# Weights of a two-layer linear-attention kernel asked for behind a copy on POOL, the last key sums one chunk later, and a layer norm's transposes all on DVE

## The chip, the cores and the metric

The kernel runs on one core of a Trainium2 chip. The time is the device time of one execution in microseconds (us), the median of several. Before the change three runs gave 2497.05 us as the median, 2494.74 to 2499.38.

## The reference

A row matrix x of 2048 x 576 goes through two layers, each an attention block and a dense block, with the same weights in both layers:

```
x = x + A(layernorm(x))      # 32 heads of 18: q, k, v = x @ wqkv
                             # phi(p) = [softmax(p), softmax(-p)], p = q @ w_phi or k @ w_phi, per head
                             # o = phi_q (phi_k^T v) / (phi_q . sum(phi_k) + 1e-6);  A = o @ wo
x = x + B(layernorm(x))      # h = relu(x @ w1 + b1)^2 (4608 wide);  B = h @ w2 + b2
```

All of it is float32. phi_k^T v and the sum of phi_k run over all 2048 rows, so a layer's attention outputs cannot begin before all of its keys are done.

## The kernel before, in words

**Numbers.** Each operand of a matrix product is split into a high part (rounded to fp32r) and a low part (the rest), and three products (high x high, high x low, low x high) stand for one. So each weight is held as two pieces, and PE (TensorE, the matmul engine) does nearly all of the work.

**Tiles and stages.** The rows come in four blocks of 512, each of four row tiles of 128. The kernel folds w_phi into the query and key weights, makes the keys of all blocks (`opening`), and then runs the dense blocks of the row blocks one after the other, in layer 0 in the order 3, 2, 0, 1 (tiles m_3, m_2, m_0, m_1), then `between` and layer 1. A dense block (`g_mlp`) loops over 36 chunks of 128 hidden features. A chunk f has 14 matmuls into ph (L975, the hidden layer), ReLU and square on ACT (ScalarE) into a tile hr (L980, L981; tag "hr", two buffers), a split of hr on DVE (VectorE) into hb (L984, L985), and, one chunk later, 12 matmuls by rows (L1000) and 3 for the last 128 columns (L992) into the accumulators. The chunk's weights come from DRAM through SP's DMA queue: m_h (640 KB, L938) into two buffers, asked for when the chunk two before has used its buffer, and m_s (576 KB, L950) likewise.

**What is woven in.** Between the steps of a dense block other work is put: a `Plan` holds calls with a turn and a depth, and `weave` runs one slot of it after each of the block's 72 yields. Turn n is slot 2n + 1, so about one turn passes for each chunk. In layer 0's dense block i the plan holds (a) for i < 3 the attention of the next row block (`plan_attend`): attention weights, their way through DRAM and back ("trips": stored by ACT's DMA queue as small pieces, fetched again in another order, and turned in 32 x 32 blocks by DVE, tiles z, phs and e), the output projection `out.project` (L816) with the output weights "o", and the layer norm of its result; and (b) for i > 0 the keys and values of layer 1 for the row block just finished (`plan_keys`): a layer norm, key products with weights "k" from turn 4 on, value products with weights "v" from turn 4.5 on, and the sums phi_k^T v (`kv_tile`, L593, 64 short matmuls a row tile) at turns 8.5 (row tiles 0 and 1) and 10.5 (2 and 3).

**How weights are asked for.** `asked` (L302) makes the calls that load a weight: four pieces, two halves times high and low, each one DMA on SP's queue (two for "o": the first four head groups, and a small one for the last), into tiles of two buffers for each of two tags. Key and output weights share the tags "wraw" and "rr" (TAGS_C); value weights share "whi" and "wlo" (TAGS_A) with the trips of blocks i > 0. The programs of PE, ACT, DVE and POOL (GpSimd) stand in the order in which they are written. SP's does not: its order is settled when the program is built, by when each DMA's buffer and data are reckoned to be ready, and on the chip it is kept. So a load whose buffer has long been free is issued early, and an issue that has to wait holds all behind it.

**The layer norm's transposes.** In the attention of blocks i > 0 and of layer 1 the normalised rows go through DRAM as well (`TripNorm`: DRAM tiles xrm, and xrt for the last 64 columns): `store` (L419, L422) and `fetch` (L430, L432) on ACT's queue, `flip` (L437) on DVE. In layer 0's first dense block only three of the four row tiles do, without their last 64 columns; the fourth tile and all four tails are transposed by PE (`Norm.turn` L384, `Norm.rest` L393, tiles a_2np).

## Time and profile before

| | |
|---|---|
| median of three runs | 2497.05 us (2494.74 to 2499.38) |
| the profiled execution, time | 2497.19 us |
| its span, first to last instruction | 2495.5 us |
| PE busy | 2478.5 us, 99% |
| DVE, ACT, POOL busy | 1260.1, 788.1, 189.4 us |
| moved by DMA | 545.07 MB, 218 GB/s on the mean |
| granted PE clock | 1.00 |

How to read the rows that follow in the prediction. A list of waits gives: engine, tile and line, "<-" who ended the wait, us in total, how many times, the longest. A timeline row gives the start, how long it took, engine, line, operation, out<-in tiles, and, in brackets, the engine's idle time before it and who ended it. A chain row gives a start and a length. A row of windows gives the stretch, its length, the busy time of PE, PEld (PE's weight loads), DVE, ACT and POOL (each with its count), the granted clock, the DMA engines' busy share and GB/s. SPq and ACTq are the DMA issues of those engines' queues; "issue" means that the engine waited for nothing that the profile shows. PE's ends are modelled, and a matmul starts before the modelled end of the one ahead of it.

### The profile page before, as it was taken

Reading aid. Unit: us, or ns where it says so; the run is one execution under the profiler, and the core shown is the slowest. Engines: PE = TensorE matmul, PEld = TensorE weight load, DVE = VectorE, ACT = ScalarE, POOL = GpSimd, SP = SyncE. Lnnn points to the kernel's source line nnn. Section 1 sums busy time; section 2 is a strip of 40 time slices with the busy share of each in tenths; the row PEclk is TensorE's granted clock in tenths of the full one; section 3 lists DMA queues with packets and bytes.
Section 4 is the critical chain, followed back from the end, with each engine's and each line's share of the span. In section 5 each row is a group of like instructions: output and inputs, shape, how many; then the busy total and the mean of one; then the engine's idle time right before and its main releaser. Section 6 shows DMA issues by size and latency. Waiting matters only on the chain.

```text
span 2495.5 us, 37635 instructions
## 1 busy us (share of the span) xinstructions
PE 2478.5 (99%) x14968; PEld 2182.9 (87%) x14968; DVE 1260.1 (50%) x2214; ACT 788.1 (32%) x1439; POOL 189.4 (8%) x539
## 2 busy tenths in 40 slices
PE   9999999999999999999999999999999999999999
PEld 8999888888888888888888988888888888888887
DVE  6679885545744476455113776433453436442112
ACT  5444453422232223223213332413233222312212
POOL 4211100000200001000000011000110002000000
PEclk9999999999999999999999999999999999999999
DMA  9313698986767677684565248678576867676565
GB/s 321 98 54 92 243 315 266 310 315 205 259 229 271 217 206 273 216 298 146 195 199 182 92 141 263 209 217 291 186 257 204 261 219 246 217 230 230 194 199 171
DMA packets 214374, 545.07 MB, mean 218 GB/s; under 512 B 29006, under 2 KB 96814, under 8 KB 214198
## 3 DMA queue, kind: packets, MB, share of 16 engines
q1 hardware_dynamic: 163638, 500.44, 60.8%
q10 hardware_dynamic: 50560, 42.21, 5.3%
q8 instruction: 119, 1.95, 0.3%
q14 instruction: 57, 0.47, 0.1%
HBM read 439.20 MB, written 103.38 MB: 217 GB/s over the span
## 4 chain that ended last, share of the span: by engine, by line
PE 95%; DMA 2%; DVE 1%; ACT 1%; issue 1%; SPq 0%; ACTq 0%; DVEq 0%
PE m_1ph L975 9%; PE m_3ph L975 9%; PE m_0ph L975 9%; PE m_2ph L975 9%; PE m_1acc L1000 7%; PE m_3acc L1000 7%; PE m_2acc L1000 7%; PE m_0acc L1000 7%; PE m_1acc L992 2%; PE m_3acc L992 2%; PE m_2acc L992 2%; PE m_0acc L992 2%; PE a_0po L816 1%; PE a_2po L816 1%; PE kvp L593 1%; PE a_3po L816 1%
## 5 line engine op out<-in xcount | busy, mean ns | idle before, releaser
L975 PE MATMUL m_2ph<-a_2nh,m_2h 128*128 128x512 f32 x720 | 225.2, 394 | 1.2 <-ACT m_2hr L980 0.7
L975 PE MATMUL m_0ph<-a_0nh,m_0h 128*128 128x512 f32 x720 | 225.0, 394 | 1.3 <-ACT m_0hr L980 1.1
L1000 PE MATMUL m_3acc<-m_3s,m_3hb 128*128 128x448 f32 x864 | 189.3, 367 | 0.4 <-DVE m_3hb L984 0.4
L1000 PE MATMUL m_1acc<-m_1s,m_1hb 128*128 128x448 f32 x864 | 189.0, 367 | 0.3 <-PE m_1ph L975 0.3
L1000 PE MATMUL m_2acc<-m_2s,m_2hb 128*128 128x448 f32 x864 | 188.9, 367 | 0.0
L1000 PE MATMUL m_0acc<-m_0s,m_0hb 128*128 128x448 f32 x864 | 188.8, 367 | 0.0
L984 DVE CAST m_2hb<-m_2hr 128x512 fp32r<-128x512 f32 x72 | 31.2, 433 | 292.4 <-ACT m_2hr L981 292.3
L1000 PEld LDWEIGHTS m_1acc<-m_1s,m_1hb 128*128 128x128 f32 x864 | 161.9, 188 | 18.8 <-PE m_1ph L975 0.5
L1000 PEld LDWEIGHTS m_3acc<-m_3s,m_3hb 128*128 128x128 f32 x864 | 161.2, 188 | 17.8 <-PE m_3ph L975 0.6
L1000 PEld LDWEIGHTS m_2acc<-m_2s,m_2hb 128*128 128x128 f32 x864 | 161.6, 188 | 17.2
L1000 PEld LDWEIGHTS m_0acc<-m_0s,m_0hb 128*128 128x128 f32 x864 | 161.6, 188 | 17.2
L975 PEld LDWEIGHTS m_2ph<-a_2nh,m_2h 128*128 128x128 f32 x720 | 135.3, 188 | 32.7 <-ACT m_2hr L980 1.2
L975 PEld LDWEIGHTS m_0ph<-a_0nh,m_0h 128*128 128x128 f32 x720 | 135.2, 188 | 32.8 <-ACT m_0hr L980 1.5
L984 DVE CAST m_1hb<-m_1hr 128x512 fp32r<-128x512 f32 x72 | 30.7, 427 | 258.8 <-ACT m_1hr L981 258.8
L980 ACT ACTIVATE m_2hr<-m_2ph,b1t 128x512 f32<-128x512 f32 x72 | 49.6, 689 | 339.1 <-PE m_2ph L975 327.4
L980 ACT ACTIVATE m_1hr<-m_1ph,b1t 128x512 f32<-128x512 f32 x72 | 49.6, 689 | 319.1 <-PE m_1ph L975 309.1
L980 ACT ACTIVATE m_0hr<-m_0ph,b1t 128x512 f32<-128x512 f32 x72 | 49.6, 689 | 317.2 <-PE m_0ph L975 288.6
L984 DVE CAST m_0hb<-m_0hr 128x512 fp32r<-128x512 f32 x72 | 31.5, 438 | 229.0 <-ACT m_0hr L981 229.0
L984 DVE CAST m_3hb<-m_3hr 128x512 fp32r<-128x512 f32 x72 | 31.7, 440 | 173.6 <-ACT m_3hr L981 173.6
L980 ACT ACTIVATE m_3hr<-m_3ph,b1t 128x512 f32<-128x512 f32 x72 | 49.6, 689 | 219.3 <-PE m_3ph L975 209.2
L975 PE MATMUL m_3ph<-t0onh,m_3h 128*128 128x512 f32 (+1 forms) x380 | 112.9, 384 | 0.6 <-ACT t0onh L385 0.5
L975 PE MATMUL m_1ph<-t1onh,m_1h 128*128 128x512 f32 (+1 forms) x380 | 112.4, 382 | 0.8 <-ACT t1onh L385 0.5
(2050 smaller groups left out, 5734.9 us busy)
## 6 DMA issues: line engine op xcount, KB each, us to landing
m_2h<-dw SPq DMA_DIRECT2D x72, 640.0 KB
m_0h<-dw SPq DMA_DIRECT2D x72, 640.0 KB
m_1h<-dw SPq DMA_DIRECT2D x72, 640.0 KB
m_2s<-dw SPq DMA_DIRECT2D x72, 576.0 KB
m_0s<-dw SPq DMA_DIRECT2D x72, 576.0 KB
m_1s<-dw SPq DMA_DIRECT2D x72, 576.0 KB
dw<-m_3h SPq DMA_DIRECT2D x36, 640.0 KB
m_3h<-dw SPq DMA_DIRECT2D x36, 640.0 KB
```

The source lines that it names most:

```text
L593: nc.tensor.matmul(po[32 * q : 32 * q + 32, :, j], vt[:, h * VW : h * VW + 32], e[:, :, h * DH : (h + 1) * DH], start=not stay, stop=True, ...
L816: nc.tensor.matmul(pt[:, :HP], a, m[:w, g], start=(g == 0 and k == 0), stop=(g == NG - 1 and k == 2))
L975: nc.tensor.matmul(ph[:, cols], a, m, start=(k == 0), stop=(k == 3 * KC + 1))
L980: nc.scalar.activation(hr, ph, AF.Relu, bias=b1t[:, f : f + 1])
L984: nc.vector.tensor_copy(hh, hr)
L992: nc.tensor.matmul(acc[KC], a, m, start=(f == 0 and k == 0), stop=(f == NF - 1 and k == 2))
L1000: nc.tensor.matmul(acc[t][:, :R], a[:, rows], m, start=(f == 0 and k == 0), stop=(f == NF - 1 and k == 2))
```

## The change

Four edits.

1. `asked` gets a flag `paced`. With it, ahead of each piece's DMA POOL copies one number into the piece's tile, from `beat["now"]`, the hr tile that was squared last. The DMA writes over that number, so it may not start before the copy, and the copy not before the square. It is on for "o" in layer 0's blocks i > 0 and for all key and value weights of `plan_keys`. The copy touches the first column of the first head group only, so the small DMA of each "o" piece has nothing to wait for.
2. The key weights of `plan_keys` for the third and fourth block are asked for at turns 32 to 35 of the block before (`keyw`), and then the value weights at turns 0 to 3 (8 to 11 in the last block, as before). In the second block both are asked for in its own first turns, as before.
3. The second sum of keys moves from turn 10.5 to 11.5.
4. In layer 0's first dense block all four row tiles and their tails now go through DRAM and DVE. Their fetches stand two turns later than before; the fourth tile is scaled sooner.

```diff
+    beat = {}
+
-    def asked(which, name, tags=TAGS_A):
+    def asked(which, name, tags=TAGS_A, paced=False):
...
+            if paced:
+                nc.gpsimd.tensor_copy(pair[half][k][0:1, 0, 0:1], beat["now"][0:1, 0:1])
             for d, piece in moved(which, half, k, pair[half][k]):
                 nc.sync.dma_start(piece, d)
...
-        trips = range(NT if whole else NT - 1)
-        norm = TripNorm(dst, f"{name}n", b, out.keep, trips, whole)
-        more = 0 if queries else 2
-        scales = [at + 1, at + 2, at + 3, at + 4 if whole else at + 5.5 + more]
+        norm = TripNorm(dst, f"{name}n", b, out.keep, range(NT), True)
+        more = 0 if queries else 2 if whole else 4
+        scales = [at + 1, at + 2, at + 3, at + 4]
...
             nc.vector.tensor_sub(hl, hr, hh.bitcast(F32))
+            beat["now"] = hr
...
-                        o = asked("o", n2, TAGS_C)
+                        o = asked("o", n2, TAGS_C, not layer)
...
+                        keyw = asked("k", f"w1_{b}", TAGS_C, True)
+                        for n, call in enumerate(keyw[1]):
+                            plan.put(at + 20.5 + n, 9, call)
...
-        (vw, vcalls), (kw, kcalls) = asked("v", f"w{m}"), asked("k", f"w{m}", TAGS_C)
+        vw, vcalls = asked("v", f"w{m}", TAGS_A, True)
+        kw, kcalls = keyw or asked("k", f"w{m}", TAGS_C, True)
         for n in range(4):
-            plan.put(8 + n if last else 2 + n / 2, 9, vcalls[n])
-            plan.put(n / 2, 9, kcalls[n])
+            plan.put(8 + n if last else n if keyw else 2 + n / 2, 9, vcalls[n])
+            if not keyw:
+                plan.put(n / 2, 9, kcalls[n])
...
-                plan.put(8.5 + t // 2 * 2, 3, add, t)
+                plan.put(8.5 + t // 2 * 3, 3, add, t)
```

What this moves, at three places of the programs. First SP's queue at the head of layer 0's second dense block. m_2h_4 is chunk 4's w1 weight, m_2s_3 chunk 3's w2 weight; w_3k0l is the low piece of the first half of the key weights, w_3v1h the high piece of the second half of the value weights. Before:

```order
L938 DMA m_2h_2_6316<-dw_2_143 128x1280
L938 DMA m_2h_3_6339<-dw_3_144 128x1280
L950 DMA m_2s_2_6318<-dw_2_179 128x1152
L310 DMA w_3k1l<-kept_kl 128x1440
L938 DMA m_2h_4_6403<-dw_4_145 128x1280
L310 DMA w_3v0l<-kept_vl 128x1440
L950 DMA m_2s_3_6378<-dw_3_180 128x1152
L310 DMA w_3v1h<-kept_vh 128x1440
L938 DMA m_2h_5_6462<-dw_5_146 128x1280
```

After the change:

```order
L941 DMA m_2h_2_6318<-dw_2_143 128x1280
L941 DMA m_2h_3_6343<-dw_3_144 128x1280
L314 DMA w_3k0h<-kept_kh 128x1440
L953 DMA m_2s_2_6320<-dw_2_179 128x1152
L314 DMA w_3k0l<-kept_kl 128x1440
L314 DMA w_3k1h<-kept_kh 128x1440
L314 DMA w_3k1l<-kept_kl 128x1440
L953 DMA m_2s_3_6383<-dw_3_180 128x1152
L314 DMA w_3v0h<-kept_vh 128x1440
L941 DMA m_2h_4_6409<-dw_4_145 128x1280
```

Before, m_2h_4 has one key piece ahead of it behind m_2s_2 (three key pieces and a value piece stood in the block before); now it has three key pieces, m_2s_3 and a value piece there, and the first key piece stands ahead of m_2s_2.

The same place in POOL's program (n_3d is the layer norm's reciprocal deviation of one row tile, two operations each). Before:

```order
L359 TENSOR_SCALAR n_3d_6284<-n_3m_6283 128x1
L360 TENSOR_TENSOR n_3d_6284<-n_3d_6284,mhalf 128x1
L359 TENSOR_SCALAR n_3d_6292<-n_3m_6291 128x1
L360 TENSOR_TENSOR n_3d_6292<-n_3d_6292,mhalf 128x1
L359 TENSOR_SCALAR n_3d_6335<-n_3m_6334 128x1
L360 TENSOR_TENSOR n_3d_6335<-n_3d_6335,mhalf 128x1
L359 TENSOR_SCALAR n_3d_6399<-n_3m_6398 128x1
L360 TENSOR_TENSOR n_3d_6399<-n_3d_6399,mhalf 128x1
```

After the change:

```order
L312 CAST w_3k0h<-m_2hr_6272 1x1
L363 TENSOR_SCALAR n_3d_6286<-n_3m_6285 128x1
L364 TENSOR_TENSOR n_3d_6286<-n_3d_6286,mhalf 128x1
L363 TENSOR_SCALAR n_3d_6294<-n_3m_6293 128x1
L364 TENSOR_TENSOR n_3d_6294<-n_3d_6294,mhalf 128x1
L312 CAST w_3k0l<-m_2hr_6272 1x1
L312 CAST w_3k1h<-m_2hr_6272 1x1
L363 TENSOR_SCALAR n_3d_6339<-n_3m_6338 128x1
L364 TENSOR_TENSOR n_3d_6339<-n_3d_6339,mhalf 128x1
L312 CAST w_3k1l<-m_2hr_6360 1x1
L312 CAST w_3v0h<-m_2hr_6360 1x1
```

The copies stand between the norms of the row tiles: the second and third piece behind the norms of two tiles, the fourth behind that of the third. The first three read the square of chunk 1 (m_2hr_6272), the next two that of chunk 2.

Last SP's queue where the output weights come in the second block (a_0o0h is the high piece of the first half; 126x1152 is the DMA of the first four head groups, 72x288 the small one). Before:

```order
L310 DMA a_0o0h<-kept_oh 72x288
L310 DMA a_0o0l<-kept_ol 126x1152
L938 DMA m_2h_10_6999<-dw_10_151 128x1280
L310 DMA a_0o0l<-kept_ol 72x288
L1491 DMA a_0qs_7404<-qs_3_128 128x576
L310 DMA a_0o1h<-kept_oh 126x1152
L950 DMA m_2s_9_6986<-dw_9_186 128x1152
L310 DMA a_0o1h<-kept_oh 72x288
L310 DMA a_0o1l<-kept_ol 126x1152
L938 DMA m_2h_11_7122<-dw_11_152 128x1280
L310 DMA a_0o1l<-kept_ol 72x288
```

After the change:

```order
L314 DMA a_0o0h<-kept_oh 126x1152
L314 DMA a_0o1h<-kept_oh 72x288
L953 DMA m_2s_13_7356<-dw_13_190 128x1152
L941 DMA m_2h_15_7423<-dw_15_156 128x1280
L314 DMA a_0o0l<-kept_ol 126x1152
L953 DMA m_2s_14_7408<-dw_14_191 128x1152
L314 DMA a_0o1l<-kept_ol 72x288
L941 DMA m_2h_16_7491<-dw_16_157 128x1280
L314 DMA a_0o1h<-kept_oh 126x1152
L953 DMA m_2s_15_7482<-dw_15_192 128x1152
L941 DMA m_2h_17_7548<-dw_17_158 128x1280
L314 DMA a_0o1l<-kept_ol 126x1152
```

Before, the pieces stood around m_2h_10 and m_2h_11, as soon as the key weights' buffers were free; now each large one stands behind another chunk's m_2h, from chunk 14's on. The small pieces of the high and low first half stay where they were.

8 lines of the change are left out of this document (4 added, 4 removed).

## Prediction

> **What bounds the kernel now.** I read the page first, then the list of waits of the matmul engine PE, then the places in the timeline that the list points to, and last the DMA windows.
>
> ```profile
> span 2495.5 us, 37635 instructions
> ## 1 busy us (share of the span) xinstructions
> PE 2478.5 (99%) x14968; PEld 2182.9 (87%) x14968; DVE 1260.1 (50%) x2214; ACT 788.1 (32%) x1439; POOL 189.4 (8%) x539
> ```
>
> PE is the bound: 2495.5 - 2478.5 = 17.0 us of the span are not matmuls. So a change that leaves the matmuls alone can win at most what PE waits. The change touches layer 0's dense blocks, and its weight loads lie between 520 and 1110 us (second and third dense block). The waits of PE in that window, all of them:
>
> ```profile
> PE kv_3k L593 <- issue: 1.2, 1, 1.2
> PE m_0ph L975 <- ACT m_0hr L980: 1.1, 1, 1.1
> PE m_2ph L975 <- ACT m_2hr L980: 0.7, 1, 0.7
> PE m_2ph L975 <- DMA m_2h<-dw: 0.5, 1, 0.5
> PE m_0ph L975 <- DMA m_0h<-dw: 0.2, 1, 0.2
> ```
>
> Five waits, 3.7 us in all. A listed wait is shorter than what it costs, since a matmul normally starts before the modelled end of the one ahead of it. In PE's timeline, the step from the last matmul group of one feature chunk to the next chunk, once without and once with a wait:
>
> ```profile
> 613.90 0.86 PE L992 MATMUL m_2acc<-m_2hb,m_2s 128*128 128x512 f32 x3
> 614.61 0.39 PE L975 MATMUL m_2ph<-a_2nh,m_2h 128*128 128x512 f32 x1
> ...
> 620.25 0.85 PE L992 MATMUL m_2acc<-m_2hb,m_2s 128*128 128x512 f32 x3
> 621.62 0.47 PE L975 MATMUL m_2ph<-a_2nh,m_2h 128*128 128x512 f32 x1 [0.51 <-DMA m_2h<-dw]
> ```
>
> The step takes 0.71 us without and 1.37 us with: 0.66 us lost for 0.51 listed, so 0.15 more for each wait. Five waits cost 3.7 + 5 x 0.15 = 4.5 us. That is what the paced loads can win.
>
> **Where those waits come from.** Mean DMA share and GB/s (last two columns) of five stretches:
>
> ```profile
> 533.00:541.50 8.50, 8.50 (x42) 7.31 (x41) 4.88 (x13) 2.86 (x5) 1.97 (x11) 1.00 1.02 403
> 594.00:622.00 28.00, 27.49 (x266) 24.01 (x266) 20.33 (x28) 9.07 (x14) 0.00 (x0) 1.00 0.97 261
> 610.00:615.00 5.00, 5.00 (x146) 4.53 (x146) 4.60 (x8) 2.67 (x4) 0.00 (x0) 1.00 1.00 239
> 636.00:662.00 26.00, 26.00 (x120) 22.20 (x120) 23.77 (x35) 7.16 (x10) 5.89 (x19) 1.00 0.82 271
> 776.00:789.00 13.00, 13.00 (x69) 11.62 (x69) 7.37 (x16) 2.40 (x4) 0.79 (x2) 1.00 1.01 357
> ```
>
> From 594 to 622 the four output-weight pieces arrive in one go on full DMA engines (0.97): the hidden weights m_2h come late at 621.62, and the 1.2 us named "issue" (PE waits for no semaphore) falls at 627, just behind the same jam. The third block's 0.2 us is the same place. From 776 to 789 three key pieces arrive on full engines (1.01), and ACT is held there (first the chain of waits, then ACT's timeline):
>
> ```profile
> 789.04 10.64 DMA xrm<-a_0nr
> ```
> ```profile
> 800.86 0.69 ACT L980 ACTIVATE m_2hr<-m_2ph,b1t 128x512 f32<-128x512 f32 x1 [6.62 <-issue]
> ```
>
> ACT may fetch the rows only when their store has landed, 10.64 us after its issue, at 799.7; the ReLU queued behind the fetch (L980) starts late, at 800.86, and PE waits 0.7 us for it (1.1 us in the third block).
>
> **The change part by part.** *All rows by DVE* (first dense block only). PE loses its transposes of the fourth row tile and of the tails. Their places in PE's timeline:
>
> ```profile
> 474.86 0.60 PE L384 MATMUL a_2np<-ident,a_2nn 128*128 128x128 f32 x4
> 475.29 0.38 PE L393 MATMUL a_2np<-ident,a_2ne 128*64 128x128 f32 x2
> 475.43 2.72 PE L1000 MATMUL m_3acc<-m_3s,m_3hb 128*128 128x448 f32 x12
> ```
>
> From start to start that is 0.57 us, and the other tail pair (0.14, as here from 475.29 to 475.43) makes 0.7 us. What comes instead, four small stores, two fetches and the 32x32 transposes, is on ACT's queue and DVE, which the page shows at 32% and 50%; the fetch now stands five turns behind its store, so ACT should not be held by it. If that cover failed, one ACT wait like the one above would come back, 0.9 us. *Key sums later* moves 64 short matmuls behind the next hidden chunk: same matmuls, no saving, no cost.
>
> *Output and key weights in pieces.* The output pieces move from the jam at 594 to four chunks from about 636 on, one per chunk; the key pieces of the third and fourth block come one per chunk behind the ReLUs of chunks 32 to 35, so that from 776 to 789 two 720 KB pieces fewer arrive. With both jams gone all five waits should go: -4.5 us. Bounds: -1.0 (only the two DMA waits, 0.7 + 2 x 0.15) to -4.5.
>
> *The head of the second block* pays. There all eight key and value pieces now come in the first chunks, where four came ahead of the block before. Each piece waits for POOL, POOL for the layer norm's sums, and SP's queue stands still meanwhile. What POOL does there (the norms of row tiles 1 and 2), ACT's square of chunk 2, which the fourth piece's copy reads, and two issues on SP's queue, chunk 4's m_2h and chunk 3's m_2s:
>
> ```profile
> 532.06 0.65 POOL L360 TENSOR_TENSOR n_3d<-n_3d,mhalf 128x1 f32<-128x1 f32 x1
> ...
> 534.89 0.64 POOL L360 TENSOR_TENSOR n_3d<-n_3d,mhalf 128x1 f32<-128x1 f32 x1
> ```
> ```profile
> 534.39 0.63 ACT L981 ACTIVATE m_2hr<-m_2hr 128x512 f32<-128x512 f32 x1
> ```
> ```profile
> 533.67 0.32 SPq L938 DMA_DIRECT2D m_2h<-dw  x1
> ...
> 536.80 0.32 SPq L950 DMA_DIRECT2D m_2s<-dw  x1
> ```
>
> The first key piece goes after chunk 1's square. The second and third stand behind the norm of two row tiles: 532.06 + 0.65 = 532.7, with a copy and the issue about 533.0. The fourth stands behind the next tile's norm and chunk 2's square (535.5), then m_2s_3, which is not free before 536.8, the first value piece, and only then m_2h_4: about 537.6 instead of 533.67. Sizes, in KB of 1024 bytes:
>
> ```profile
> m_2h<-dw SPq DMA_DIRECT2D x3, 640.0 KB
> m_2s<-dw SPq DMA_DIRECT2D x3, 576.0 KB
> w_3k1l<-kept_kl SPq DMA_DIRECT2D x1, 720.0 KB
> ```
>
> From 533.0 the queue has four pieces, m_2s_3 and m_2h_4 to move: 4 x 720 + 576 + 640 = 4096 KB = 4.19 MB. At the 403 GB/s of 533 to 541.5 that takes 10.4 us, up to 543.4. To this comes the time that a lone DMA needs beyond its bytes: SP's wait for the landing of a 288 KB store,
>
> ```profile
> SPq L1062 <- DMA xm<-a_0x: 7.2, 3, 3.0
> ```
>
> is 2.4 us on the mean, its bytes 0.7 us, and the issue is a little ahead, so about 2 us (an estimate). m_2h_4 lands near 545.4. PE wants it where it starts chunk 4, and the same chunk in the third block:
>
> ```profile
> 544.01 0.47 PE L975 MATMUL m_2ph<-a_2nh,m_2h 128*128 128x512 f32 x1
> ```
> ```profile
> 835.27 0.47 PE L975 MATMUL m_0ph<-a_0nh,m_0h 128*128 128x512 f32 x1
> ```
>
> That is a new wait of 1.4 us at 403 GB/s, and of 2.7 us at the 357 of the other full stretch (4.19 MB in 11.7 us). The 1.3 MB of the first piece and m_2s_2, issued from about 529 on, may not quite be through by 533.0, up to 0.7 us more. Between 1.4 and 3.4 I take 2.3 us: the 403 row is these very loads, with some of the rest. Behind chunk 4 come key products, which need no m_2h, so the delay is paid once. In the third block only value pieces come at the head: two of them, m_0s_3 and m_0h_4 are 2656 KB = 2.72 MB from about 824.3 on (291.3 us later than 533.0), 6.7 us and 2 us, landing at 833 to 834: no wait, 0 to 1.
>
> *The copies themselves.* 32 copies of one element; POOL's nearest rows are copies of 64 and of 8 columns:
>
> ```profile
> 634.51 0.24 POOL L727 COPY a_0z<-a_0Q0e 128x64 f32<-128x64 f32 x1
> 634.68 0.19 POOL L728 COPY a_0z<-a_0Q0e 128x8 f32<-128x8 f32 x1
> ```
>
> POOL is 8% busy. The number read (hr) has two buffers, so ACT's ReLU two chunks later waits for the copy; the longest queue ahead of a copy is the rearranging of one tile's weights (12 operations, at the 636 to 662 row's 5.89 / 19 = 0.31 us each 3.7 us) against two chunks, 12.7 us (614.61 to 621.62, less the 0.66 lost, twice). I cost this at nothing; if a copy came late by more than that cover, PE would wait for the ReLU.
>
> **The sum.** -4.5 - 0.7 + 2.3 = -2.9 us. The profiled execution took 2497.19 us, 0.14 above the median of 2497.05, so the forecast is 2497.05 - 2.9 = 2494.2 us. Two timings of this kernel can be told apart from about 0.2% (5 us) on; the runs shown spread over 4.6 us.
>
> **The rivals.** *The head drains in time.* If PE is not kept waiting at chunk 4, only the gains stay: -5.2, 2491.9 us, just past 0.2%. For it: single stretches at 533 to 541.5 ran above 403; against it: m_2h_4 is issued four us later with four pieces ahead. [...]
>
> *The output weights meet the attention trips.* From 636 to 662 the engines already carry 271 GB/s at share 0.82, mostly stores and fetches of attention weights. Four pieces of 648 KB add 2.65 MB in 26 us, 102 GB/s: 373 in all, share 1.1 at that stretch's own efficiency. A queue of up to 0.13 x 26 = 3.4 us would build, against a slack that the list of waits does not show. If it cost 1.5 us in each block: -2.9 + 3.0, 2497.2 us.
>
> *The jam only moves, and is dearer (slower).* If the eight pieces at the head drain like the output pieces did, at the 239 GB/s of 610 to 615, m_2h_4 needs 17.5 us and lands at 552.5: a wait of 8.5 us, and in the third block 11.4 us, 837.7, 2.4 us. Then 10.9 - 5.2 = +5.7, 2502.8 us. It decides from 10.2 us of new waits on, a drain below 245 GB/s. Against it: key and value pieces did move at 403 before; it is the output pieces that are slow.
>
> *It does not do what it says.* The "issue" wait and the two ReLU waits stay where they are: 3.0 + 3 x 0.15 = 3.5 us less gain, +0.6, 2497.6 us. For it: none of the three names a weight load. [...]
>
> **How the numbers follow.** Forecast 0.36, head drains in time 0.24, output weights collide 0.15, jam dearer 0.12, no effect on the three waits 0.13. Faster by over 0.2% is the first rival, 0.24; slower by over 0.2% the third, 0.12; the other cases lie within, 0.64. The range leaves out the jam: its low end is 2491.9 less the 1.4 us by which a gain could be sized too small, 2490.5; its high end is the collision or the no-effect case with the new wait at 3.4 instead of 2.3 us and 1 us in the third block, 2500.0.
>
> **What would show it.** Right: the five waits missing from PE's list, none at 594 to 630, and one new wait of 1 to 4 us for m_2h at chunk 4 of the second block; no a_2np matmuls. Wrong: PE waiting for ReLUs behind POOL's copies, a wait for m_2h or m_2s at chunks 14 to 18, or ACT still held ten us by the last row fetch.

## The result and the profile after

The change is slower. Four runs of the kernel after have a median of 2513.03 us (2511.48 to 2515.34), four of the kernel before 2496.68 us (2494.74 to 2499.38): a ratio of 1.0065, with a 95% interval from 1.0048 to 1.0083. The forecast was 2494.2, its range ended at 2500.0. The profiled execution took 2514.03 us, and its page begins:

```profile
span 2512.3 us, 37716 instructions
...
PE 2483.8 (99%) x14960; PEld 2184.4 (87%) x14960; DVE 1265.8 (50%) x2217; ACT 789.6 (31%) x1439; POOL 198.0 (8%) x571
```

PE has eight instructions fewer than before and yet is busy 5.3 us longer (2483.8 against 2478.5), and outside its matmuls the span is 28.5 us instead of 17.0. So there are two losses, waits and slower matmuls. PE's waits in the kernel after (lines have moved by 3 or 4: L978 is the hidden matmuls, L983 the ReLU, L1004 the second matmuls by rows, L996 those for the last 128 columns):

```profile
PE m_2ph L978 <- DMA m_2h<-dw: 3.2, 1, 3.2
PE m_2ph L978 <- ACT m_2hr L983: 3.2, 2, 2.5
PE m_0ph L978 <- ACT m_0hr L983: 2.6, 2, 1.4
PE m_2acc L996 <- DMA m_2s<-dw: 1.6, 1, 1.6
PE m_0acc L1004 <- DVE m_0hb L987: 1.6, 2, 0.8
...
PE m_2acc L1004 <- DMA m_2s<-dw: 1.0, 1, 1.0
```

The first is the wait that the prediction expected at the head. The "issue" wait at 627 us is gone; the waits for ReLUs are longer than before, and waits for feature pieces and for DVE have joined them. Three transfers now stand in the chain of waits of the second block, with their start and length:

```profile
537.69 9.45 DMA m_2h<-dw
...
657.54 16.58 DMA phs<-a_0z
...
812.00 6.62 DMA m_2s<-dw
```

The stretches that the prediction showed, in the kernel after (the last three columns are granted clock, DMA share, GB/s):

```profile
533.00:541.50 8.50, 8.50 (x43) 7.35 (x42) 4.73 (x13) 3.10 (x5) 2.39 (x6) 1.00 0.97 350
594.00:622.00 28.00, 28.00 (x275) 25.00 (x275) 18.49 (x24) 8.16 (x13) 0.00 (x0) 1.00 0.48 154
636.00:662.00 26.00, 26.00 (x211) 22.32 (x201) 20.92 (x29) 7.18 (x10) 7.40 (x28) 1.00 0.92 287
776.00:789.00 13.00, 13.00 (x76) 11.91 (x76) 6.79 (x17) 1.32 (x2) 0.79 (x2) 1.00 0.77 253
```

The bytes moved as planned: the jam of 594 to 622 went from share 0.97 to 0.48, that of 776 to 789 from 1.01 to 0.77, and 636 to 662 filled from 0.82 to 0.92 on the mean.

**Where the time went, by place.** I cut the second and the third dense block at the start of PE's hidden matmuls of chunks 9, 13 and 21 and took the lengths from PE's timeline of one profiled execution of each kernel. The pieces are the head (chunks 0 to 8), the stretch of the old jam (9 to 12), the attention trips (13 to 20) and the rest, with the block's end (21 to 35). First the lengths before, then the differences to before, in us; the last column is the measured ratio less one, times 2497 us.

```
                second block                third block               whole
                head  jam trips  end        head  jam trips  end      run
before          86.1 30.7  51.1 123.5       86.1 28.9  51.1 124.1
after           +5.0 -2.1  +6.1  +1.7       +1.4 -0.3  +4.4  +0.7    +16.2
all_free        +1.5 -1.8   0.0  -1.2        0.0 +1.0   0.0  -1.8     -0.7
pace_only       +6.2 -2.1  +7.5  -1.2       +5.0 -0.3  +6.8  -1.8    +18.5
o_free          +5.9 -2.1   0.0  +1.8       +0.4 -0.4   0.0  +0.8     +6.7
kv_free         +1.8 -2.0  +8.2  +0.2        0.0 -0.3  +3.4   0.0     +4.7
keyw_free       +3.2 -2.1  +4.2  -1.2       +1.2 -0.3  +3.5  -1.8    +10.0
copy_const      +5.8 -2.1  +0.3  -1.2       +0.7 -0.4  +1.3  -1.4     +4.2
pool_issue      +0.5 -2.0  +7.6  +0.7       +0.1 -0.3  +6.5  -0.6    +13.7
head_act        +3.3 -2.1  +6.8  +1.1       +1.2 -0.4  +4.5  +0.5    +14.7
warm16          +3.4 -2.1  +7.9  +4.8       +0.8 -0.3  +4.0  +0.7    +14.2
o_late          +6.7 -2.0   0.0  +5.2       +0.5 -0.3   0.0  +1.4     +7.0
late_free       +1.9 -2.1   0.0  +0.1        0.0 -0.3   0.0  -1.2     -2.5
before_late     -0.1 -2.1   0.0  +0.5        0.0 -0.3   0.0  -0.6     -0.7
sums_only       -0.1 -1.6   0.0  +0.5        0.0 +0.9   0.0  +0.2     +0.5
rows_only       +2.1 -2.1   0.0  +0.5        0.0 +0.2   0.0  -0.9     +0.2
late_best       -0.1 -2.2   0.0  -1.2        0.0 -0.3   0.0  -0.6     -2.2
```

In the kernel after, the eight pieces sum to 16.9 us. The first dense block is 0.7 us shorter (259.3 to 258.6), and the layers behind are as they were (1393.6 and 1393.7 us from the fourth block on). Three places lose: head, trips, end. One profile of a kernel is one execution: *o_free*, *keyw_free* and *o_late* below have the same program in the second block's head as the kernel after, and that head runs from +3.2 to +6.7 in the four profiles; the second block's trips, with the same program in *after*, *kv_free*, *keyw_free*, *head_act* and *warm16*, run from +4.2 to +8.2. So only differences beyond such a spread are read from the table.

**The slower matmuls.** At two places the granted clock is halved. Ahead of and behind the wait at the head, and ahead of and behind the wait of 2.5 us at 676:

```profile
544.70:548.00 3.30, 0.72 (x3) 0.66 (x4) 1.66 (x4) 0.01 (x1) 0.00 (x0) 1.00 1.01 421
548.10:551.40 3.30, 3.30 (x9) 2.63 (x8) 0.00 (x0) 0.00 (x0) 0.00 (x0) 0.50 1.02 420
674.40:677.70 3.30, 1.30 (x6) 1.07 (x7) 1.86 (x3) 2.37 (x3) 0.00 (x0) 1.00 0.77 216
677.80:681.10 3.30, 3.30 (x10) 2.53 (x9) 3.23 (x4) 0.00 (x0) 0.00 (x0) 0.50 0.99 340
```

Each costs about 1.6 us more: eight matmuls at 0.20 us over their usual step (0.43 instead of 0.23 us from one start to the next). Nothing of this kind was in the kernel before, or in the prediction.

### The profile page after: what moved, and what is told of

It is laid out like the page before. It is cut to its first block, busy times and chain, and to the rows that moved or that the text cites. A ratio compares the mean times of both kernels' runs of the same rounds, so it can differ in the third digit from the quotient of the medians.

```text
span 2512.3 us, 37716 instructions
## 1 busy us (share of the span) xinstructions
PE 2483.8 (99%) x14960; PEld 2184.4 (87%) x14960; DVE 1265.8 (50%) x2217; ACT 789.6 (31%) x1439; POOL 198.0 (8%) x571
## 4 chain that ended last, share of the span: by engine, by line
PE 92%; DMA 4%; issue 2%; DVE 1%; ACT 1%; POOL 0%; SPq 0%; ACTq 0%; DVEq 0%; POOLq 0%
PE m_1ph L978 9%; PE m_3ph L978 9%; PE m_2ph L978 9%; PE m_0ph L978 8%; PE m_1acc L1004 7%; PE m_3acc L1004 7%; PE m_2acc L1004 6%; PE m_0acc L1004 6%; PE m_1acc L996 2%; PE m_3acc L996 2%; PE m_2acc L996 2%; PE m_0acc L996 2%; PE a_2po L820 1%; PE a_0po L820 1%; DMA phs<-a_0z 1%
## 5 line engine op out<-in xcount | busy, mean ns | idle before, releaser
L978 PE MATMUL m_2ph<-a_2nh,m_2h 128*128 128x512 f32 x720 | 227.6, 398 | 6.5 <-DMA m_2h<-dw 3.2
L978 PE MATMUL m_0ph<-a_0nh,m_0h 128*128 128x512 f32 x720 | 225.1, 394 | 3.7 <-ACT m_0hr L983 2.6
L1004 PE MATMUL m_0acc<-m_0s,m_0hb 128*128 128x448 f32 x864 | 189.5, 367 | 1.7 <-DVE m_0hb L987 1.6
L1004 PE MATMUL m_2acc<-m_2s,m_2hb 128*128 128x448 f32 x864 | 189.3, 367 | 1.1 <-DMA m_2s<-dw 1.0
L1004 PE MATMUL m_3acc<-m_3s,m_3hb 128*128 128x448 f32 x864 | 189.3, 367 | 0.4 <-DVE m_3hb L987 0.4
L1004 PE MATMUL m_1acc<-m_1s,m_1hb 128*128 128x448 f32 x864 | 189.0, 367 | 0.4 <-PE m_1ph L978 0.4
L1004 PEld LDWEIGHTS m_0acc<-m_0s,m_0hb 128*128 128x128 f32 x864 | 161.3, 188 | 20.3 <-DVE m_0hb L987 2.5
L1004 PEld LDWEIGHTS m_1acc<-m_1s,m_1hb 128*128 128x128 f32 x864 | 161.9, 188 | 18.8 <-PE m_1ph L978 0.5
L1004 PEld LDWEIGHTS m_2acc<-m_2s,m_2hb 128*128 128x128 f32 x864 | 161.4, 188 | 19.2 <-issue 1.4
L1004 PEld LDWEIGHTS m_3acc<-m_3s,m_3hb 128*128 128x128 f32 x864 | 161.4, 188 | 18.0 <-PE m_3ph L978 0.6
L978 PEld LDWEIGHTS m_2ph<-a_2nh,m_2h 128*128 128x128 f32 x720 | 136.8, 190 | 38.7 <-ACT m_2hr L983 4.1
L978 PEld LDWEIGHTS m_0ph<-a_0nh,m_0h 128*128 128x128 f32 x720 | 135.2, 188 | 35.4 <-ACT m_0hr L983 3.4
L983 ACT ACTIVATE m_2hr<-m_2ph,b1t 128x512 f32<-128x512 f32 x72 | 49.6, 689 | 335.9 <-PE m_2ph L978 309.4
L983 ACT ACTIVATE m_1hr<-m_1ph,b1t 128x512 f32<-128x512 f32 x72 | 49.6, 689 | 321.2 <-PE m_1ph L978 316.2
L983 ACT ACTIVATE m_0hr<-m_0ph,b1t 128x512 f32<-128x512 f32 x72 | 49.6, 689 | 309.6 <-PE m_0ph L978 295.8
L983 ACT ACTIVATE m_3hr<-m_3ph,b1t 128x512 f32<-128x512 f32 x72 | 49.6, 689 | 216.8 <-PE m_3ph L978 206.7
L978 PE MATMUL m_2ph<-a_2nl,m_2h 128*128 128x512 f32 x288 | 114.0, 396 | 0.0
L978 PE MATMUL m_3ph<-t0onh,m_3h 128*128 128x512 f32 (+1 forms) x380 | 112.9, 384 | 0.6 <-ACT t0onh L389 0.5
```

Source lines behind the costliest of these rows:

```text
L978: nc.tensor.matmul(ph[:, cols], a, m, start=(k == 0), stop=(k == 3 * KC + 1))
L983: nc.scalar.activation(hr, ph, AF.Relu, bias=b1t[:, f : f + 1])
L1004: nc.tensor.matmul(acc[t][:, :R], a[:, rows], m, start=(f == 0 and k == 0), stop=(f == NF - 1 and k == 2))
```

## The experiments

**All of the holding back, and nothing else of the change.** *all_free* takes `paced` away from every call; *pace_only* is the kernel before with the copies alone.

```diff
 all_free, against the change:
-                        o = asked("o", n2, TAGS_C, not layer)
+                        o = asked("o", n2, TAGS_C)
-                        keyw = asked("k", f"w1_{b}", TAGS_C, True)
+                        keyw = asked("k", f"w1_{b}", TAGS_C)
-        vw, vcalls = asked("v", f"w{m}", TAGS_A, True)
-        kw, kcalls = keyw or asked("k", f"w{m}", TAGS_C, True)
+        vw, vcalls = asked("v", f"w{m}", TAGS_A)
+        kw, kcalls = keyw or asked("k", f"w{m}", TAGS_C)
```

> The changed kernel with no copy at all: what stays of the change is that the first three dense blocks' rows are scaled by DVE on all four tiles, the last key sums half a turn to a turn later, and the third block's key pieces asked for one block ahead. Theory 1 (all of the loss is the pacing): the time of before less the 0.6 us that the first dense block gained, 2496 to 2497, and no stretch of half clock. Theory 2 (the early key pieces of the third block, or the later key sums, carry part of the loss: they bring bytes into the block's last turns): 2499 to 2504, the waits at the block's end (810 and 818 us, 2.7 us) stay.

> The kernel before with the pacing alone: rows, key sums and the third block's key pieces as before, the pieces of keys, values and output weights of the second layer's preparation held back by the copy. Theory 1 (all of the loss is the pacing): the time of the change plus the 0.6 us that the transposes cost, 2512 to 2515, with the wait of 3.4 us and its half clock in the second block's head and the waits at 663 to 676 us. Theory 2 (part of the loss comes from the other edits): 2500 to 2509, and where the difference to the change shows, by block, says which.

Measured: *all_free* 2497.09 us, ratio 0.9997 (0.9988 to 1.0006); *pace_only* 2517.65 us, ratio 1.0074 (1.0061 to 1.0088). So the copies carry the whole loss, theory 1 for both. What PE waits for at the three places is gone in *all_free*; its list names only these in the two blocks:

```profile
PE m_2ph L978 <- DMA m_2h<-dw: 1.4, 1, 1.4
PE m_0ph L978 <- DMA m_0h<-dw: 1.1, 1, 1.1
```

*pace_only* came out above its 2515, because its third block pays a head of its own (+5.0 us): there the key pieces too are asked for in the head, which the early request of the change spares.

**One group of pieces at a time.** *o_free* undoes the first of the lines above alone, *kv_free* the others alone, *keyw_free* only the `keyw` line.

> The changed kernel with one thing undone: the output weights of the second and third dense block are asked for without the copy that holds each piece back. Theory 1 (collision: the held-back output weights now load at 636 to 680 us, beside the attention trips' store of the phases' tile 1, which took 16 us, and the ReLU and the half-clock stretch at 676 us come from that): the waits at 663.30, 670.03 and 676.10 us (1.14 + 0.25 + 2.65 us) and the half clock behind the last (1.5 us) go, 5.6 us, the old jam at 594 to 627 us comes back with the 2.1 us it cost before; in the third block 4.4 us of the waits at 846.92 to 977.28 us go and 0.3 come back. Sum: 7.6 us faster than the change, some 2505.4. Theory 2 (the loss is that of all pacing together, a shift of all that SP issues, not of the output weights' place): the waits at 663 to 676 us stay in some form, the time is within 2 us of the change's 2513.0.

> The changed kernel with the copies ahead of the key and value pieces undone, in the second, third and fourth block; output weights still held back, the third block's key pieces still asked for in turns 32 to 35 of the block before. Theory 1 (the paced key and value pieces make the head: 4.19 MB ahead of m_2h_4, which then misses its matmul by 3.4 us, and the clock at 0.50 for 3.4 us behind that wait): the 3.4 us wait at 546.97 us and the half clock (1.55 us) go, and the third block's 1.3 us at 846.92; some 6.3 us faster than the change, 2506.7, with PE's clock back to 0.999 in the second block's head. Theory 2 (the head's feature pieces are late by the queue of SP as such, whatever the key pieces do): wait and half clock stay, time within 1.5 us of the change's.

> The changed kernel with one copy group undone: the third and fourth block's key pieces, asked for in the last turns of the block before, go without a copy. Theory 1 (at the block's end these pieces, held until 795 to 815 us, load beside the stores of the row trips, whose last fetch then comes 9.5 us behind its store; with the constant copied the pieces went at 785 to 800 us and the fetch came 6.4 us behind): the end's waits (0.91 + 1.80 us in the second block, 1.36 + 0.89 us in the third) go, 4 to 5 us faster than the change, 2508 to 2509. Theory 2 (the end is late because the trips start late, after the losses at 663 to 676 us): they stay, within 1.5 us of the change.

Measured: *o_free* 2505.15 us, 1.0027 (1.0017 to 1.0038); *kv_free* 2504.53 us, 1.0019 (1.0009 to 1.0029); *keyw_free* 2508.11 us, 1.0040 (1.0027 to 1.0052). Theory 1 in all three, and the table puts each gain where it belongs: without held-back output weights the trips cost 0.0 in both blocks; without held-back keys and values the second head falls to +1.8 and the third to 0.0; without held-back early keys the ends go from +1.7 and +0.7 to -1.2 and -1.8. The 2.1 and 0.3 us that *o_free* was expected to lose again in the old jam did not come back (-2.1, -0.4), so that the median's closeness to 2505.4 is luck in part: by the ratios 9.5 us were won, not 7.6. *kv_free* won more than expected, as the ends gained too (+0.2 and 0.0). The profile of *keyw_free* is that of its fastest execution (2502.81 us), and its lower head and trips belong to that execution.

**Why the output weights hurt.** ACT's timeline at the trips in the kernel after; ACTq L736 stores a tile, L743 fetches it rearranged:

```profile
657.08 0.93 ACTq L736 DMA_DIRECT2D phs<-a_0z  x2
...
674.22 0.35 ACTq L743 DMA_DIRECT2D a_0e<-phs  x1
674.61 1.16 ACT L557 ACTIVATE a_0Q3e<-a_0Q3e 128x1152 f32<-128x1152 f32 x1 [10.59 <-DMA phs<-a_0z]
675.68 0.67 ACT L983 ACTIVATE m_2hr<-m_2ph,b1t 128x512 f32<-128x512 f32 x1
```

The fetch goes 17.1 us after the store's issue, and the exponential and the ReLU of the chunk stand behind it on ACT's queue. The same store, fetch and ReLU before (L732, L739, L980):

```profile
654.34 0.93 ACTq L732 DMA_DIRECT2D phs<-a_0z  x2
...
660.79 0.34 ACTq L739 DMA_DIRECT2D a_0e<-phs  x1
...
666.32 0.69 ACT L980 ACTIVATE m_2hr<-m_2ph,b1t 128x512 f32<-128x512 f32 x1 [2.57 <-PE m_2ph L975]
```

There the fetch went 6.5 us after the store, and ACT had 2.6 us to spare ahead of the ReLU. The DMA engines at this place, in the kernel after and then before (the last two columns are share and GB/s):

```profile
648.00:672.00 24.00, 22.94 (x103) 18.76 (x102) 18.06 (x25) 5.13 (x7) 7.98 (x26) 1.00 1.02 329
```
```profile
648.00:672.00 24.00, 24.00 (x110) 20.45 (x109) 22.55 (x33) 6.72 (x9) 5.91 (x18) 1.00 0.90 302
```

So the engines were full while the store was on its way; the 0.92 of 636 to 662 is a mean over a slacker first half and this. *o_late* asks for the same pieces, with the same copies, eight turns later, behind the trips:

```diff
-                            plan.put(at + n, 9, call)
+                            plan.put(at + 8 + n, 9, call)
```

> The changed kernel with the held-back output weights asked for eight turns later, behind the attention trips of the second and third dense block instead of beside them. Theory 1 (collision: what costs 5.6 and 4.4 us in the two blocks is that these bytes load while the store of the phases' tile and the fetch behind it run): those waits go and the old jam at 594 to 627 us doesn't come back; 9 to 10 us faster than the change, 2503 to 2504, or 1 to 2 us faster than with the output weights not held back at all. Theory 2 (the bytes cost wherever they are put, since each turn's SP queue is as full): the waits move with them to 710 to 760 us, time within 3 us of the change.

```profile
658.08 0.93 ACTq L736 DMA_DIRECT2D phs<-a_0z  x2
...
666.49 0.34 ACTq L743 DMA_DIRECT2D a_0e<-phs  x1
666.88 1.17 ACT L557 ACTIVATE a_0Q3e<-a_0Q3e 128x1152 f32<-128x1152 f32 x1 [1.85 <-DMA phs<-a_0z]
670.07 0.69 ACT L983 ACTIVATE m_2hr<-m_2ph,b1t 128x512 f32<-128x512 f32 x1 [2.02 <-PE m_2ph L978]
```

Here the fetch goes 8.4 us after the store, and ACT still has 2.0 us to spare ahead of the ReLU. The trips cost 0.0 in both blocks, which is the collision (theory 1). In time it measured 2506.38 us, 1.0028 (1.0017 to 1.0040), 2.4 us above what that theory gave, though by the two ratios to before it won 9.2 us, as forecast: head and end were dearer in its profile (+6.7 and +5.2 against +5.0 and +1.7, the end with a half clock of its own, 0.93 on the mean from 800 to 825 us).

**What the block's end loses.** The row trips end with a store and a fetch of the same kind, and here the kernel after is no slower than before. The last store of rows and its fetch, before and then after:

```profile
789.04 0.37 ACTq L419 DMA_DIRECT2D xrm<-a_0nr  x1
...
799.77 0.34 ACTq L430 DMA_DIRECT2D a_0nn<-xrm  x1
```
```profile
797.87 0.99 ACTq L423 DMA_DIRECT2D xrm<-a_0nr  x1
...
808.41 0.36 ACTq L434 DMA_DIRECT2D a_0nn<-xrm  x1
```

That is 10.7 us before and 10.5 us after, and PE's wait for the ReLU behind the fetch is as it was (0.72 and 0.75 us; in the third block 1.11 and 1.19). Where the key pieces are not held back (*all_free*), the fetch goes 6.0 us after its store and that wait is gone. So holding them back kept the old wait. The new loss is a wait of 1.65 us at 818.76 for a w2 piece, m_2s, which stands on SP's queue behind a key piece that waits for its copy until 811.59:

```profile
811.59 0.32 SPq L314 DMA_DIRECT2D w_2k1h<-kept_kh  x1
812.00 0.38 SPq L953 DMA_DIRECT2D m_2s<-dw  x1
```

In the third block the same wait is 0.72 us, and in *keyw_free* neither block has it.

**What holds the pieces in the head.** *copy_const* keeps all copies, but their number comes from the constant identity, so that they wait for no ReLU:

```diff
-    beat = {}
+    beat = {"now": ident}
-            beat["now"] = hr
```

> The changed kernel in which each copy takes its number from the constant identity instead of from the latest ReLU's tile: the copies and their semaphores stay on POOL and SP, the wait for a new number goes. Theory 1 (the loss is the holding back, not the copies, of 0.17 to 0.73 us each on an engine that nobody waits for): the time with no copies at all, 2495 to 2499, and no half clock. Theory 2 (POOL's copies and SP's waits for POOL cost by themselves, since POOL's queue reaches them late): over 2503, and PE waits in the head of the second block for m_2h as in the change.

It measured 2501.78 us, 1.0017 (1.0008 to 1.0027), between the two theories, and the table says why: trips and ends are nearly clean (+0.3, +1.3, -1.2, -1.4), the head is not (+5.8). POOL's timeline there, with the constant:

```profile
531.73 0.65 POOL L364 TENSOR_TENSOR n_3d<-n_3d,mhalf 128x1 f32<-128x1 f32 x1
532.34 0.18 POOL L312 CAST w_3k0l<-ident 1x1 fp32r<-1x1 f32 x1
...
535.08 0.17 POOL L312 CAST w_3k1l<-ident 1x1 fp32r<-1x1 f32 x1
```

In the kernel after the same two copies stand at 532.52 and 535.26. They wait in POOL's queue behind the layer norm's steps (L364), which wait for DVE's sums, whatever the copies read. *head_act* turns it round: the head's eight copies are made by ACT, behind its own ReLU, and POOL's queue has no part in it.

```diff
+            if paced == "act":
+                nc.scalar.activation(pair[half][k][0:1, 0, 0:1], beat["now"][0:1, 0:1], AF.Copy)
-            if paced:
+            elif paced:
```

> The changed kernel with the head's eight copies (keys and values of the second block) made by ACT right behind its ReLU instead of by POOL, where they stand behind the row norm's steps that wait for DVE (copies at 532.52, 535.26, 541.71 us; with a constant as the number copied, still at 532.34, 535.08, 540.70). Theory 1 (POOL's order, not the wait for a new number, sets when these pieces are issued): the pieces go out 2 to 4 us earlier, m_2h_4 lands earlier, the wait of 3.4 us falls under 2.5 us and the clock stays at 1.00: 2 to 4 us faster than the change, 2509 to 2511. Theory 2 (the wait for the number would hold them as long by itself): wait over 3 us, clock 0.50 behind it, time as the change's.

The second and third piece went out 2 us earlier (counted from the block's start), m_2h_4 within 0.3 us of the change's, and PE waited as long (3.14 us idle against 3.25): theory 1 falls. Theory 2 had the wait and the time, but not the clock, which stayed at 1.00. The time was 2512.41 us, 1.0059 (1.0046 to 1.0072). What sets m_2h_4's issue in all three kernels is the order of SP's queue, where m_2h_4 now stands behind m_2s_3. With the constant and then with ACT's copies:

```profile
536.37 0.32 SPq L953 DMA_DIRECT2D m_2s<-dw  x1
...
537.43 0.43 SPq L941 DMA_DIRECT2D m_2h<-dw  x1
```
```profile
537.93 0.32 SPq L955 DMA_DIRECT2D m_2s<-dw  x1
...
538.78 0.43 SPq L943 DMA_DIRECT2D m_2h<-dw  x1
```

m_2s_3 has to wait until PE has used its buffer, and it goes 16.2 us after the block's start in these two, in the kernel after and in the kernel before alike (the blocks start at 520.21, 521.77, 520.38 and 520.55). Before, m_2h_4 stood ahead of it. So neither the wait for the number nor POOL's turn makes m_2h_4 late; the place that it got in SP's order does. That SP's queue is what matters, and not the bytes, shows when POOL issues the pieces itself (*pool_issue*):

```diff
-                nc.sync.dma_start(piece, d)
+                (nc.gpsimd if paced else nc.sync).dma_start(piece, d)
```

> The changed kernel with the held-back pieces issued by POOL, right behind its copy, instead of by SP: the pieces come as late as before, but SP goes on to the feature pieces without waiting for the copy. Theory 1 (in the head the loss is that SP's queue is held, so that m_2h_4 is issued 4 us late; at the trips it is the bytes themselves beside the store): the 3.4 us wait and its half clock in the head shrink to under 1.5 us in all, the waits at 663 to 676 us and 967 to 977 us stay; 3 to 5 us faster than the change, 2508 to 2510. Theory 2 (only the bytes count, wherever they are issued): the waits stay in both places, within 1.5 us of the change. Theory 3 (only SP's order counts, at the trips too): both go, 2499 to 2503.

SP's queue in the head, first in the kernel after, then with POOL issuing:

```profile
532.72 0.32 SPq L314 DMA_DIRECT2D w_3k0l<-kept_kl  x1
533.13 1.46 SPq L314 DMA_DIRECT2D w_3k1h<-kept_kh  x1
536.01 0.32 SPq L314 DMA_DIRECT2D w_3k1l<-kept_kl  x1
536.54 0.32 SPq L953 DMA_DIRECT2D m_2s<-dw  x1
536.95 0.69 SPq L314 DMA_DIRECT2D w_3v0h<-kept_vh  x1
537.69 0.73 SPq L941 DMA_DIRECT2D m_2h<-dw  x1
```
```profile
534.17 0.44 SPq L941 DMA_DIRECT2D m_2h<-dw  x1
```

m_2h_4 stands ahead of m_2s_3 again (536.87) and goes 3.5 us earlier, PE's idle time ahead of it falls from 3.25 to 0.36 us and the head from +5.0 to +0.5; the trips stay (+7.6, +6.5). That is theory 1 by place. In time the gain was only 2.5 us by the ratios (2512.56 us, 1.0055, 1.0043 to 1.0068), below the 3 to 5 expected, and the two intervals overlap. The trips were dearer in its profile than in the change's; whether POOL's issuing made them so was not tested.

**Is the half clock a price of idling?** *warm16* puts 16 transposes of the identity into the wait of the head; their result is not used.

```diff
+        def warm():
+            pt = wtile(f"warm{m}")
+            for i in range(16):
+                nc.tensor.transpose(pt[:, i % NT * P : (i % NT + 1) * P], ident, ident)
+
+        if not keyw:
+            plan.put(3, -5, warm)
```

> The changed kernel with 16 extra transposes of 128x128 by PE just ahead of the second block's chunk 4, where PE waited 3.4 us for m_2h_4 and the granted clock was 0.50 for 3.4 us behind it. They use nothing that is late, and lie inside the wait, which they cut in two. Theory 1 (the clock falls because PE stood idle for over some 2 us; it did not behind the wait of 1.8 us at 818 us): no half clock there, the eight matmuls behind at 0.20 us less each, 1.6 us faster than the change in that block. Theory 2 (the clock falls for another reason, such as the transfers at that place): clock 0.50 for 3.4 us as before, no gain, or up to 1 us of loss by the transposes.

PE's timeline and the windows of that kernel at the place:

```profile
544.45 1.97 PE L1541 MATMUL warm<-ident 128*128 128x128 f32 x16 [1.19 <-DVE n_3l L390]
546.44 0.47 PE L978 MATMUL m_2ph<-a_2nh,m_2h 128*128 128x512 f32 x1
```
```profile
548.00:552.00 4.00, 4.00 (x21) 3.49 (x20) 0.63 (x1) 1.32 (x2) 0.60 (x1) 1.00 0.77 312
```

The clock stays at 1.00 and the head costs +3.4 instead of +5.0, which is theory 1's 1.6 us. But the transposes are not shown to have done it: *keyw_free*, without them, waits 3.0 us at the same place, keeps its clock (1.000 on the mean of the run) and has +3.2. The transfers, theory 2's example, are not the reason either, since *head_act* and *keyw_free* had the same ones there and kept their clock. The whole run did not gain for certain (2513.45 us, 1.0057, 1.0045 to 1.0070): in its profile the clock fell at two other places, to a mean of 0.88 from 662 to 674 us and of 0.93 from 800 to 825, where PE was idle for 2.0 and 3.9 us in all, and the end cost +4.8.

**A version that beats both.** *late_free* joins *kv_free* and *o_late*; *before_late* is the kernel before with the later key sums and the late output weights alone; *late_best* is *late_free* with the first block's rows as before.

> The changed kernel with keys and values not held back and the output weights held back until behind the attention trips (eight turns later). Theory 1 (each loss has its own place, and the three are the head, the trips and the block's end): only the wait of 1.5 us that the kernel with no copy at all has at 532 us stays, its 1.2 us at 912 us goes; 2495 to 2497, the before's 2498 less 1 to 3 us. Theory 2 (held-back weights cost wherever they land): 2499 to 2502.

> The kernel before with two things alone: the last key sums a turn later, and the output weights of the second and third dense block held back until behind the attention trips. Theory 1: of the 4.6 us of waits that PE has in these blocks before, 0.67 + 1.40 + 0.33 us at 594 to 627 and 912 us go, those at the blocks' ends (0.88 and 1.28 us) stay; 2495 to 2497, 1 to 3 us under before. Theory 2 (held-back weights cost wherever they land): 2499 to 2502.

> The fastest kernel so far (no copies but on output weights behind the trips) with the first dense block's rows as before, so that the fourth row tile is transposed by PE again. Theory 1 (the rows by DVE cost the head 1.9 us and win 0.7 us): 1 us faster than that one, 2492 to 2494, 0.15% under before. Theory 2 (they cost nothing in the head): 0.7 us slower, 2494 to 2496.

Measured: *late_free* 2494.17 us, 0.9990 (0.9981 to 0.9998); *before_late* 2495.72 us, 0.9997 (0.9988 to 1.0005); *late_best* 2495.49 us, 0.9991 (0.9982 to 1.0000). *before_late* is inside theory 1's range, though its interval includes no gain, and *late_free* is 0.8 us below its own. *late_free* is the one whose interval lies below before, by some 2.5 us; *late_best*, with nearly no wait left in the two blocks (its profile has -3.4 and -0.9 us there), was not told apart from it; its time lies in theory 2's range, so the 1 us of gain was not shown.

**What took the old waits.** The waits at 594 to 630 us are gone in every kernel above, held back or not. Two edits alone, on the kernel before: the later key sums (*sums_only*), and the rows by DVE, the fourth edit of the change as it stands in the diff there (*rows_only*).

```diff
 sums_only:
-                plan.put(8.5 + t // 2 * 2, 3, add, t)
+                plan.put(8.5 + t // 2 * 3, 3, add, t)
```

> The kernel before with the last key sums a turn later, and nothing else. Theory 1 (this edit, not the holding back, took the waits of the second block at 594 to 630 us: they are gone in every changed kernel, held back or not): that stretch is 2.0 us shorter than before, all else as before; 2494 to 2497. Theory 2 (the early key pieces or the rows did it): the waits of 0.67 and 1.40 us stay, time as before.

> The kernel before with all four row tiles of the first dense block scaled by DVE, and nothing else. Theory 1 (this edit costs the 1.5 to 1.9 us that the kernels without held-back keys lose in the head of the second block at 530 us, since the extra stores and fetches delay SP's pieces there): first block 0.7 us shorter, that head 1.5 us longer, 2496 to 2498. Theory 2 (the head's loss comes from the key pieces' order alone): first block 0.7 us shorter, head as before, 2495 to 2497, and the head's stretch of 86.1 us unchanged.

Measured: *sums_only* 2497.69 us, 1.0002 (0.9993 to 1.0011); *rows_only* 2497.40 us, 1.0001 (0.9992 to 1.0010). Later key sums shorten the second block's stretch by 1.6 us (the "issue" wait is gone), with 0.9 us more in the third block's, and *rows_only* by 2.1 us, though its head loses the same 2.1 us to a wait for m_2h at 532 us; that a block which runs two microseconds later finds its pieces there is argued, not shown. *pace_only* has neither edit and shortens the stretch by 2.1 us as well. So each of the three edits alone clears most of it, and holding back was not needed for it; what the "issue" wait was for stays open. Both theories on *sums_only* hold in part (the rows do it too), theory 1 on *rows_only* holds in the head. Its 0.7 us of gain in the first block is not in its profile (259.8 us); over the seventeen profiles, the block takes 258.6 us on the median with the rows by DVE and 259.4 without.

## Why the prediction was wrong

The forecast was the sum -4.5 - 0.7 + 2.3. By place the kernel after measured -2.4 at the two jams, -0.7 in the first block, +6.4 in the two heads, +10.5 in the two trips and +2.4 at the two ends: 16.2 us.

**The trips stood at nothing in the sum.** They were a rival, at 0.15 and 1.5 us per block: "the output weights meet the attention trips". They lost 6.1 and 4.4 us, more than any other place, and the loss vanishes when the same pieces come eight turns later. The step that failed is the price of that meeting. The prediction spread the pieces over 26 us (102 GB/s on top of 271, a share of 1.1) and bounded the delay by a queue of 3.4 us. The engines were indeed full, at 1.02 from 648 to 672 us; but one store that others wait for was held far longer than that bound: 17.1 us from its issue to the fetch, against 6.5 us before and 8.4 us with the pieces moved away. ACT had 2.6 us to spare there before. Behind the fetch stood the exponential and the ReLU, and PE waited 2.5 us for the ReLU, with a half clock behind; another 1.0 us, at 663, was for a w2 piece. The prediction noted "a slack that the list of waits does not show"; it was to be read from ACT's timeline of before, in the idle time ahead of the ReLU. Why this one store was held for so long by the pieces beside it, the runs do not show.

**The head was right in its mechanism, and too small.** Forecast: m_2h_4 issued at 537.6 behind m_2s_3, landed at 545.4, a new wait of 2.3 us between 1.4 and 3.4. Measured: issued at 537.69, landed at 537.69 + 9.45 = 547.1, a loss of 3.4 us at that matmul. The rate is the part that was off: 350 GB/s in 533 to 541.5 where before had 403, so 0.45 MB more were still to come at the end of that stretch, an estimated 1.1 us at the 421 GB/s behind it. PE's idle time ahead of that matmul was 3.25 us, with the engines at a share of 0.97 to 1.02. Missing altogether was the clock, 1.6 us on top: 5.0 in all. In the third block 0 to 1 was forecast and 1.4 lost.

**The block's end was taken for a gain.** I counted the two ReLU waits at the end as gone, because fewer key pieces would arrive at 776 to 789. There were fewer (share 0.77), but they came at 795 to 815 instead, beside the last row trip, and the two waits stayed as they were. For these two the rival "it does not do what it says" was right, and so was the sign that the prediction named, "ACT still held ten us by the last row fetch". On top came the w2 piece behind a held key piece, so that the ends lost 1.7 and 0.7 us where the same pieces, not held back, win 1.2 and 1.8 (*keyw_free*).

**The gains came, but not from where I took them.** 2.4 us at the two jams (-2.1 and -0.3) is what the three waits there were priced at (0.5 + 1.2 + 0.2 us, and 0.15 for each). In the second block they came without any copy too; in the third *all_free* lost 1.0 us there. The transposes brought 0.7 us in the first block, as forecast, but the rows by DVE also cost the second block's head 1.5 to 2.1 us where nothing else is late there; that edit was costed at nothing beyond the transposes. Of the key sums the prediction said "no saving, no cost": by place they shortened one stretch by 1.6 us and lengthened the next block's by 0.9, and the whole run shows neither (1.0002).

**The copies.** Costed at nothing, as POOL is 8% busy. With a constant as their number they still cost some 5 us against no copies (1.0017 against 0.9997), nearly all in the head, where m_2h_4 stands behind m_2s_3 in SP's order in each kernel whose copies hold the key pieces on that queue. I had that order in the head's sum; the general statement that a small copy on an idle engine is free was wrong.

One sum is off by little: by its own terms the range's high end is 2499.7 us (2497.6 + 1.1 + 1), not 2500.0.

## What to carry to other kernels

Before moving a transfer into a stretch with a share of 0.8 (0.82 here, from 636 to 662 us), look not only for room in bytes but for the store, fetch and compute chain that runs there, and read its slack as the idle time ahead of the next needed instruction on the waiting engine. A wait put ahead of one DMA holds every DMA behind it on that queue, as it held m_2s at the block's end (PE waited 1.65 us), and it can change the order in which the queue is built, as in the head. So look at what stands behind it, and try the same bytes from another queue or a few turns later before giving up the idea. If several edits come in one change, time each alone: here the copies lost all of the 16 us, and the best version, with copies on the output weights alone and a later place for them, is some 2.5 us under before.

## What the runs showed of the hardware

The granted clock fell behind some of PE's waits and stayed behind others as long. In the clock records of the kernel after it falls twice ahead of the program's end, behind the waits at 547 and 676, each time to 0.50 for 3.41 us; between these it is 1.00. Waits of PE and the clock behind them:

| kernel, PE's wait | us | granted clock |
|---|---|---|
| *after*, for m_2h, to 547.28 | 3.25 | 0.50 from 548.1 to 551.4 |
| *after*, for the ReLU, to 676.40 | 2.49 | 0.50 from 677.8 to 681.1 |
| *after*, for m_2s, to 818.76 | 1.65 | 1.00 from 818 to 822 |
| *o_late*, for m_2h in the head | 3.6 | 0.50 from 547 to 552 |
| *head_act*, for m_2h, to 548.56 | 3.14 | 1.00 from 548.7 to 552.1 |
| *head_act*, the longest for DVE | 2.5 | 1.000, mean of the run |
| *keyw_free*, for m_2h in the head | 3.0 | 1.000, mean of the run |

One stretch of 3.41 us at 0.50 would take the mean of a run of 2500 us to 0.9993 (an estimate), so the last two rows had none. *head_act* at the head:

```profile
548.56 0.47 PE L980 MATMUL m_2ph<-a_2nh,m_2h 128*128 128x512 f32 x1 [3.14 <-DMA m_2h<-dw]
```
```profile
548.70:552.10 3.40, 3.40 (x16) 2.80 (x17) 0.00 (x0) 0.04 (x1) 0.00 (x0) 1.00 1.03 417
```

So the length of a wait alone does not tell: 2.49 us had a half clock behind it in the kernel after, 3.14 us none in *head_act*. What else decides is not shown. Each fall in the kernel after, whose PE is 99% busy, cost 1.6 us on top of its wait, and the wait of *head_act* nothing.
